# Second MoE of a three-stage kernel: one branch over two experts, the small second product ahead of it, row loads on another queue, small tiles at other addresses

## The chip, the cores and the metric

The kernel runs as one program on one core of one Trainium2 chip. The metric is device time in microseconds (us), from the first to the last instruction of one execution; lower is better. Of the core's engines five matter here: TensorE (PE, matrix products; PEld is its loading of weights), VectorE (DVE), ScalarE (ACT), GpSimd (POOL, which also issues the indirect DMAs) and SyncE (SP, which here issues the plain DMAs). Each engine runs its own list of instructions in order, branches included, and engines wait for each other through semaphores.

## The reference, cut to what matters

The program computes three things in a row: linear attention, a dense mixture of experts (every token through all eight experts), and a second mixture of experts with routing. Only the last is changed.

```
def _moe2_ref(x, w_gate, w1, w2, capacity):          # N 1152 tokens, D 512, E 8, F 1024, capacity 288
    logits = x @ w_gate
    expert_idx = np.argmax(logits, axis=1)
    ...                                              # gate_w: softmax probability of the expert taken
    for i in range(N):                               # the first `capacity` tokens of an expert get a slot
        e = expert_idx[i]
        if counts[e] < capacity:
            disp[e, counts[e]] = x[i]
            ...
    h = np.maximum(np.einsum('ecd,edf->ecf', disp, w1), 0.0)
    y = np.einsum('ecf,efd->ecd', h, w2)
    for i in range(N):
        if keep[i]:
            out[i] = gate_w[i] * y[expert_idx[i], pos[i]]
```

## The kernel before, in words

The first two stages keep TensorE busy and leave the tokens in the SBUF tile `acc` (128 x 9 x 520 values). Routing then writes each token's row, with its gate and its number behind it, to a DRAM buffer `disp` of 8 x 288 slots: nine indirect DMAs that POOL issues (L723), with the slot numbers in the small tile `slot_i`. They read `acc` and `slot_i` until they have landed. A bit mask `many` says which experts have more than 32 tokens.

The second MoE treats each expert in two parts. The small part takes the first 32 slots of an expert and always runs, in four steps for each expert. `first_small` (L1048, 32 matmuls) multiplies the 32 rows by w1; `relu_small` (L1056, ACT) applies the ReLU into a tile `g`; `turn_small` transposes (L1062, 2 matmuls) and copies (L1064, DVE) into `h`; `second_small` (L1072, 64 matmuls) multiplies by w2. Then `out_small` (L1079, ACT) scales by the gate, and `rows_out` (L1030, POOL) scatters the result to the output. The rows of four experts lie together in one tile: for experts 0 to 3 it is built before this stage, for experts 4 to 7 it is loaded by `slots_load` (L900) and transposed by `slots_trans` (L1020).

The large part, `large`, takes slots 32 to 287 of an expert and runs only under a branch on that expert's bit (`tc.If`, L1172). It loads 2 x 128 rows (`rows_load`, L1025), transposes them (L1100, 8 matmuls), and splits rows and weights into a high and a low part (ACT cast L80, then DVE subtract L81). The first product is 96 matmuls (L1113), the second 48 (L1130 to L1132), and ACT and DVE scale the two halves (L1138, L1136). Before the change the branch has two sides, and `second_small` is in both: inside `large`, behind the transposes of the rows, and alone in the other side. The loop over experts runs `turn_small(e)`, `out_small(e-1)`, `first_small(e+1)`, the branch of e, `relu_small(e+1)`. In the profiled data the experts 2 and 6 have more than 32 tokens; the other six skip the large part.

The weights come as 64 pieces of 512 KB (`load`, L535, on SP's queue), eight for each expert. There is room for 36 pieces; `done(e)` gives back the eight places of expert e, and the next `load(64)` fills all that are free.

The order is written out by hand: in this stage each engine runs its instructions as the code lists them. What sets the order is therefore the order of the lines, and a tile's address decides what its first writer waits for: a tile laid where an older tile lay waits for that tile's last readers.

Of the kernel before, what the change touches and what calls it, by code (L numbers as in the profile page):

```python
# [16 lines left out]
P = 128  # L17
# [3 lines left out]
def tile_linear_attention_two_moe(  # L21
# [507 lines left out]
    def load(n):  # L529

        while n and todo and free:
            e, i = todo.pop(0)
            src = piece(e, i)
            raws[e, i] = take((e, i), list(src.shape), F32, f"rw_{e}_{i}")
            nc.sync.dma_start(raws[e, i], wst[e, i].rearrange("p (c f) -> p c f", c=src.shape[1]))  # L535
            n -= 1

    def done(e):
        free.extend(at[e, i] for i in range(8))
# [455 lines left out]
    def bank2(k, name):  # L995
        return psum2[k].tile([P, 512], F32, tag="ps", name=name)
# [8 lines left out]
    NQD = P // C0  # L1005
    DQ = D // NQD
    tails0 = yp.tile([P, E, RW - D], F32, name="tails0")
    part = yp.tile([P, 1], F32, name="part")
    where = yp.tile([P, E], I32, name="where")
    out_q = out.rearrange("n (j d) -> (n j) d", j=NQD)  # L1010

    def slots_load(p):
        xs = yp.tile([P, D], F32, tag="xs", bufs=1, name=f"xs_{p}")
        rows_of_slots(p, xs)
        return xs
# [6 lines left out]

    def rows_load(e, c0, n):
        xs = yp.tile([P, RW], F32, tag="xt", bufs=2, name=f"xs2_{e}_{c0}")
        nc.scalar.dma_start(xs[:n, :], disp[e * cap + c0 : e * cap + c0 + n, :])  # L1025
        return xs

    def rows_out(o, at_, y, n):
# [12 lines left out]
    def first_small(e):  # L1041
        ps = bank2(0, f"q1_{e}")[:, :FP]
        x = xTs[e // EP]
        es = slice(e % EP * C0, (e % EP + 1) * C0)
        for c in range(DC):
            for j in range(NQD):
                js = slice(j * C0, (j + 1) * C0)
                nc.tensor.matmul(  # L1048
                    ps[js], x[:, c, es], raws[e, c][:, 0, j * FP : (j + 1) * FP], start=c == 0, stop=c == DC - 1,
                    tile_position=(0, j * C0),  # L1050
                )
        return ps

    def relu_small(e, ps):
        g = yp.tile([P, FP], F32, tag="g", bufs=2, name=f"g_{e}")
        nc.scalar.activation(g, ps, AF.Relu)  # L1056
        return g
# [9 lines left out]
    def second_small(e, ps, h):  # L1067
        for f in range(F // P):
            q, t = f // NH, f % NH
            for j in range(NQD):  # L1070
                js = slice(j * C0, (j + 1) * C0)
                nc.tensor.matmul(  # L1072
                    ps[js], h[:, t, q * C0 : (q + 1) * C0], raws[e, DC + f // 2][:, f % 2, j * DQ : (j + 1) * DQ],
                    start=f == 0, stop=f == F // P - 1, tile_position=(0, j * C0),
                )

    def out_small(e, ps):
        y = yp.tile([P, DQ], F32, tag="y", bufs=3, name=f"y_{e}")
        nc.scalar.mul(y, ps, tails0[:, e, 0:1])  # L1079
        rows_out(out_q, where[:, e : e + 1], y, P)  # L1080

    def large(e, chunks, rows, second):

        c0, w = chunks[0][0], sum(n for _, n in chunks)
        at_ = [c - c0 for c, _ in chunks]
# [10 lines left out]
        for c in range(0, DC, 2):  # L1096
# [4 lines left out]
                        ps[:, k, at_[i] : at_[i] + n], rows[i][:n, (c + k) * P : (c + k + 1) * P], ident[:n, :n]  # L1101
                    )
            split(xh[:, c : c + 2], xl[:, c : c + 2], ps)
        second()
        for i in range(1, DC):
            split_w(i)

# [34 lines left out]

    SETS = [REST[i : i + 2] for i in range(0, len(REST), 2)]
    assert len(SETS) <= 1
    xTs = {0: xT}
    xs = slots_load(1)
    for i in range(NQD):
        nc.sync.dma_start(
            tails0[i * C0 : (i + 1) * C0], disp[:, D:].rearrange("(e s) d -> s e d", e=E)[:C0]
        )  # L1150
    load(64)
    for j in range(NQD):
        nc.gpsimd.memset(part[j * C0 : (j + 1) * C0], float(j))
    g = relu_small(0, first_small(0))
    late = None
    for e in range(E):
        h = turn_small(e, g)
        if e == 0:
            wf = yp.tile([P, E], F32, name="wf")
            nc.vector.tensor_copy(wf, tails0[:, :, 1].bitcast(I32))  # L1160
            nc.vector.tensor_scalar(wf, wf, float(NQD), part[:, 0:1], ALU.mult, ALU.add)
            nc.vector.tensor_copy(where, wf)
        if e:
            out_small(e - 1, late)

        q = first_small(e + 1) if e + 1 < E else None
        late = bank2(0, f"q2_{e}")[:, :DQ]
        if REST:
            tc.no_sync_barrier()
            if e == 0:  # L1170
                mask = nc.values_load(many[0:1, 0:1], min_val=0, max_val=(1 << E) - 1)
            with tc.If(mask & (1 << e)) as more:  # L1172
                for chunks in SETS:
                    rows = [rows_load(e, c0, n) for c0, n in chunks]
                    large(e, chunks, rows, lambda: second_small(e, late, h))
            with more.Else():
                second_small(e, late, h)
        else:
            second_small(e, late, h)
        if q is not None:  # L1180
            g = relu_small(e + 1, q)
        if e % EP == 0 and e // EP + 1 < E // EP:
            xTs[e // EP + 1] = slots_copy(e // EP + 1, xqp, [slots_trans(e // EP + 1, xs)])
        if e:

            done(e - 1)
            load(64)
    out_small(E - 1, late)
    manual.close()


# [53 lines left out]
```

## Time and profile before

| | us |
|---|---|
| median of three runs (lowest, highest) | 1041.02 (1039.25, 1041.88) |
| the profiled execution, whole | 1043.93 |
| its span, first to last instruction | 1042.2 |
| PE busy in the span | 988.1 |
| DVE, ACT, POOL busy | 658.9, 342.7, 455.2 |

Busy time is summed over the whole span, most of which belongs to the first two stages, where PE is busy nine tenths of the time or more in nearly every slice. In the last slices, the second MoE, it is not. A row of the timeline below reads: start, duration, engine, line of the kernel, operation, output tile <- input tiles, shapes, and how many instructions the row merges; in brackets the time that the engine was idle just before, and what ended it. "issue" means that the profile shows nothing that the engine waited for.

### The profile page before, as it was taken

How to read it: one execution, taken by the hardware profiler on the slowest of the kernel's cores; microseconds unless marked ns; L12 is line 12 of the kernel's file. 1: busy time of each engine (PE TensorE's matmuls, PEld its weight loads, DVE VectorE, ACT ScalarE, POOL GpSimd, SP SyncE). 2: the span in 40 equal slices, each digit the busy share in tenths (PEclk: the TensorE clock that was granted, in tenths of full speed). 3: DMA queues.
4: the chain of work that ended last, by engine and by line, in shares of the span. 5: the costliest groups of instructions: out<-in, count | busy, mean ns of one | idle time of the engine just before them, and what ended most of it. 6: DMA issues, size and time to landing. Idle time of an engine off the chain costs nothing. (4 is left out here: it accounts for less than half of the span.)

```text
span 1042.2 us, 17368 instructions
## 1 busy us (share of the span) xinstructions
PE 988.1 (95%) x6686; PEld 889.5 (85%) x6686; DVE 658.9 (63%) x1288; ACT 342.7 (33%) x768; POOL 455.2 (44%) x480
## 2 busy tenths in 40 slices
PE   7999999999999999999999999999999999658586
PEld 7999989889998899988998889998999888537465
DVE  6766699997666666666666666666666665314041
ACT  5766553323222232332222223232223212113031
POOL 3656887646544445455544444445553300200101
PEclk9999999999999999999999999999999999868998
DMA  8888789841111111111111111111111164685500
GB/s 261 279 280 276 248 296 329 310 152 61 41 42 41 41 42 41 60 43 60 43 42 42 41 41 41 43 60 46 56 41 62 61 212 173 213 299 170 189 25 27
DMA packets 59873, 125.73 MB, mean 121 GB/s; under 512 B 6969, under 2 KB 25789, under 8 KB 59264
## 3 DMA queue, kind: packets, MB, share of 16 engines
q1 hardware_dynamic: 57904, 120.72, 34.2%
q0 software_dynamic: 1296, 2.63, 0.7%
q8 instruction: 64, 1.05, 0.4%
q10 hardware_dynamic: 576, 1.07, 0.3%
q14 instruction: 33, 0.27, 0.1%
HBM read 114.61 MB, written 44.68 MB: 153 GB/s over the span
## 5 line engine op out<-in xcount | busy, mean ns | idle before, releaser
L81 POOL TENSOR_TENSOR l<-r,h 128x256 fp32r<-128x256 f32 (+2 forms) x100 | 155.1, 1566 | 335.7 <-ACT h L80 335.7
L614 DVE SCALAR_TENSOR_TENSOR acc<-p,prob,acc 128x512 f32<-128x512 f32 x252 | 188.3, 749 | 103.0 <-PE p L605 102.9
L605 PE MATMUL p<-h,hl 128*128 128x512 f32 x576 | 226.6, 393 | 0.0
L603 PE MATMUL p<-h,hh 128*128 128x512 f32 x576 | 226.3, 393 | 0.0
L604 PE MATMUL p<-l,hh 128*128 128x512 f32 x576 | 225.1, 391 | 0.0
L569 DVE TENSOR_TENSOR ca<-ca,p 128x256 f32<-128x256 f32 (+1 forms) x256 | 113.0, 450 | 69.9 <-PE p L552 67.5
L80 ACT CAST h<-r 128x256 fp32r<-128x256 f32 (+2 forms) x108 | 70.8, 685 | 180.3 <-PE p L605 159.3
L558 ACT ACTIVATE hh<-ca 128x320 fp32r<-128x320 f32 (+1 forms) x128 | 56.3, 443 | 223.0 <-DVE ca L569 223.0
L605 PEld LDWEIGHTS p<-h,hl 128*128 128x128 f32 x576 | 108.2, 188 | 23.5 <-DVE hl L562 0.2
L604 PEld LDWEIGHTS p<-l,hh 128*128 128x128 f32 x576 | 108.2, 188 | 21.7
L603 PEld LDWEIGHTS p<-h,hh 128*128 128x128 f32 x576 | 108.3, 188 | 20.4
L81 POOL TENSOR_TENSOR lt<-t,ht 128x256 fp32r<-128x256 f32 x144 | 124.3, 891 | 1.3 <-PE pn L352 1.3
L550 PE MATMUL p<-xh,ht 128*128 128x320 f32 x256 | 79.2, 309 | 0.0
L552 PE MATMUL p<-xh,lt 128*128 128x320 f32 x256 | 79.1, 309 | 0.0
L551 PE MATMUL p<-xl,ht 128*128 128x320 f32 x256 | 79.1, 309 | 0.0
L550 PE MATMUL p<-xs,ht 128*128 128x256 f32 x256 | 72.8, 284 | 0.0
L552 PE MATMUL p<-xs,lt 128*128 128x256 f32 x256 | 72.4, 283 | 0.0
L551 PE MATMUL p<-xs,ht 128*128 128x256 f32 x256 | 72.4, 283 | 0.0
L569 DVE TENSOR_TENSOR cb<-cb,p 128x320 f32<-128x320 f32 (+1 forms) x128 | 58.1, 454 | 18.9 <-PE p L552 18.1
L562 DVE SCALAR_TENSOR_TENSOR hl<-ca,hh 128x320 fp32r<-128x320 f32 (+1 forms) x128 | 63.3, 496 | 2.3 <-ACT hh L558 1.5
L219 POOL TENSOR_TENSOR t<-r 128x256 f32<-128x256 f32 x72 | 54.8, 783 | 22.5 <-DMA r<-w1a 21.9
L562 DVE SCALAR_TENSOR_TENSOR hl<-cb,hh 128x512 fp32r<-128x512 f32 (+1 forms) x64 | 53.8, 841 | 11.0 <-ACT hh L558 11.0
(234 smaller groups left out, 2032.4 us busy)
## 6 DMA issues: line engine op xcount, KB each, us to landing
rw<-wst SPq DMA_DIRECT2D x64, 512.0 KB, 5.6
r<-w1a SPq DMA_DIRECT2D x36, 512.0 KB, 3.5
r<-w2a SPq DMA_DIRECT2D x36, 512.0 KB, 3.5
wst<-w1b SPq DMA_DIRECT2D x32, 512.0 KB, 7.1
wst<-w2b SPq DMA_DIRECT2D x32, 512.0 KB, 7.7
disp<-acc SPq DMA_DIRECT2D x18, 260.0 KB, 4.9
v<-va SPq DMA_DIRECT2D x8, 325.0 KB, 3.9
rawq<-qT SPq DMA_DIRECT2D x8, 320.0 KB, 5.6
```

The source lines that it names most:

```text
L80: nc.scalar.copy(hi, src)
L81: (eng or nc.vector).tensor_tensor(lo, src, hi, ALU.subtract)
L550: nc.tensor.matmul(ps, ws_[0], xs[0], start=i == 0, stop=False)
L551: nc.tensor.matmul(ps, ws_[0], xs[1], start=False, stop=False)
L552: nc.tensor.matmul(ps, ws_[1], xs[0], start=False, stop=i == DI - 1)
L558: nc.scalar.activation(hv[:, q0 : q0 + 2 * src.shape[1] - 1 : 2], src, AF.Relu)
L562: nc.vector.scalar_tensor_tensor(lv[:, qs], src, 0.0, hv[:, qs], ALU.max, ALU.subtract)
L569: nc.vector.tensor_tensor(o, x, ps, ALU.add)
L603: nc.tensor.matmul(ps, a, w.w2[0][:, f, :], start=f == 0, stop=False)
L604: nc.tensor.matmul(ps, a, w.w2[1][:, f, :], start=False, stop=False)
L605: nc.tensor.matmul(ps, b_, w.w2[0][:, f, :], start=False, stop=f == FT - 1)
L614: nc.vector.scalar_tensor_tensor(o, ps, prob[:, t, e : e + 1], o, ALU.mult, ALU.add)
```

## The change

Five edits, all in the second MoE. Five tiles `hi_0` to `hi_4`, used only by the large part, are now allocated before the small tiles, so that they take the addresses at which `acc` lay and the small tiles come behind. `rows_load` issues from SP instead of ACT. The loads of the first weights and the first product now stand ahead of the loads that read `disp`. `second_small` runs ahead of the branch, once. And the branch is now a tree: after every second expert one branch tests the bits of both, and inside it one branch for each runs its large part; places are given back, and weights loaded, once for a group of two.

```
+    for k in range(5):
+        yp.tile([P, 2 * D], R32, tag=f"hi{k}", bufs=1, name=f"hi_{k}")
 ...
-        nc.scalar.dma_start(xs[:n, :], disp[e * cap + c0 : e * cap + c0 + n, :])
+        nc.sync.dma_start(xs[:n, :], disp[e * cap + c0 : e * cap + c0 + n, :])
 ...
-    def large(e, chunks, rows, second):
+    def large(e, chunks, rows):
 ...
-        second()
         for i in range(1, DC):
             split_w(i)
 ...
+    GROUP = 2
     xTs = {0: xT}
+    load(64)
+    g = relu_small(0, first_small(0))
     xs = slots_load(1)
 ...
-    load(64)
 ...
-    g = relu_small(0, first_small(0))
-    late = None
+    late = {}
     for e in range(E):
         h = turn_small(e, g)
-        if e == 0:
+
+        q = first_small(e + 1) if e + 1 < E else None
+        late[e] = bank2(1, f"q2_{e}")[:, :DQ]
+        second_small(e, late[e], h)
+        if q is not None:
+            g = relu_small(e + 1, q)
+        if e == 1:
 ...
-        if e:
-            out_small(e - 1, late)
-
-        q = first_small(e + 1) if e + 1 < E else None
-        late = bank2(0, f"q2_{e}")[:, :DQ]
-        if REST:
-            tc.no_sync_barrier()
-            if e == 0:
-                mask = nc.values_load(many[0:1, 0:1], min_val=0, max_val=(1 << E) - 1)
-            with tc.If(mask & (1 << e)) as more:
-                for chunks in SETS:
-                    rows = [rows_load(e, c0, n) for c0, n in chunks]
-                    large(e, chunks, rows, lambda: second_small(e, late, h))
-            with more.Else():
-                second_small(e, late, h)
 ...
-        if e % EP == 0 and e // EP + 1 < E // EP:
+        if e % EP == 1 and e // EP + 1 < E // EP:
             xTs[e // EP + 1] = slots_copy(e // EP + 1, xqp, [slots_trans(e // EP + 1, xs)])
-        if e:
-
-            done(e - 1)
-            load(64)
-    out_small(E - 1, late)
+        if (e + 1) % GROUP == 0:
+            group = range(e + 1 - GROUP, e + 1)
+            for k in group:
+                out_small(k, late.pop(k))
+            if REST:
+                tc.no_sync_barrier()
+                if group[0] == 0:
+                    mask = nc.values_load(many[0:1, 0:1], min_val=0, max_val=(1 << E) - 1)
+                with tc.If(mask & sum(1 << k for k in group)):
+                    for k in group:
+                        tc.no_sync_barrier()
+                        with tc.If(mask & (1 << k)):
+                            for chunks in SETS:
+                                large(k, chunks, [rows_load(k, c0, n) for c0, n in chunks])
+
+            if group[0]:
+                for k in group:
+                    done(k - GROUP)
+                load(64)
```

The kernel after has five lines more; a line of the stage has grown by three (L1048 is L1051 now, L1072 is L1075), inside `large` by two or three (L1113 is L1115, L1100 is L1103).

The first place is PE at the start of the second MoE. In these rows `q_0`, `q_1` and `q_2` of L1048 are first products of experts 0, 1 and 2, `ht` a transpose, `q_0` of L1072 the second product of expert 0. Before, from the transpose of expert 0 to the one of expert 1 (the rows of `large` between the two branches left out):

```order
L1062 MATMUL ht_9853<-ident,g_9851 128x128 x2
L1048 MATMUL q_1_9862<-rw_0_9089,xT_9777 32x256 x4
...
L1171 TENSOR_LOAD many
L1172 REGISTER_ALU
L1172 COMPARE_AND_BRANCH
...
L1172 UNCONDITIONAL_BRANCH
L1072 MATMUL q_0_9879<-rw_4_9081,h_9856 32x128 x8
...
L1172 UNCONDITIONAL_BRANCH
L1020 MATMUL xst_10192<-ident,xs_9817 128x128 x4
L1062 MATMUL ht_10199<-ident,g_10190 128x128 x2
```

After, from the same transpose to the first branch:

```order
L1065 MATMUL ht_9858<-ident,g_9843 128x128 x2
L1051 MATMUL q_1_9863<-rw_0_9089,xT_9777 32x256 x4
...
L1075 MATMUL q_0_9880<-rw_4_9081,h_9861 32x128 x8
...
L1065 MATMUL ht_9915<-ident,g_9913 128x128 x2
L1051 MATMUL q_2_9920<-rw_0_9271,xT_9777 32x256 x4
...
L1075 MATMUL q_1_9937<-rw_4_9097,h_9918 32x128 x8
...
L1023 MATMUL xst_9976<-ident,xs_9845 128x128 x4
L1182 TENSOR_LOAD many
L1183 REGISTER_ALU
L1183 COMPARE_AND_BRANCH
```

The small work of two experts, and the first product of a third, now stands in one piece ahead of the first branch.

The second place is ACT at the same point, with the semaphores that each row waits for. `g` is the result of the ReLU; the semaphores DMASW0 to DMASW7 are counted up by POOL's indirect DMAs, here the scatters into `disp`. Before, the first three rows of the small part:

```order
L1056 ACTIVATE g_9851<-q_0_9834 128x256 [waits DMASW3_49,DMASW4_49,DMASW2_49,DMASW5_49,DMASW1_49,DMASW6_49,DMASW0_49,DMASW7_49,DVE_49,PE_49]
L1171 TENSOR_LOAD many [waits DVE_49]
...
L1056 ACTIVATE g_10190<-q_1_9862 128x256 [waits PE_49]
```

After:

```order
L1059 ACTIVATE g_9843<-q_0_9826 128x256 [waits DVE_49,PE_49]
L1059 ACTIVATE g_9913<-q_1_9863 128x256 [waits DMASW3_49,DMASW4_49,DMASW2_49,DMASW5_49,DMASW1_49,DMASW6_49,DMASW0_49,DMASW7_49,DVE_49,PE_49]
L1059 ACTIVATE g_9970<-q_2_9920 128x256 [waits PE_49,Activation_49]
```

The wait for all scatters has moved from the first `g` to the second, whose tile lies over `slot_i`.

The third place is SP's queue around the first loads of the stage. `rw` is a piece of the weights, `xs` (L900) and `tails` the rows and the gates read from `disp`, `xs` (L1025, L1028) the rows of a large part. Before, up to the first loads behind a branch:

```order
L535 DMA rw_1_9602<-wst 128x1024
L900 DMA xs_9817<-disp 32x512 x4
L1148 DMA tails_9814<-disp 32x8x8 x4
L535 DMA rw_2_9826<-wst 128x1024
L535 DMA rw_3_9828<-wst 128x1024
...
L1172 UNCONDITIONAL_BRANCH x2
L535 DMA rw_4_10525<-wst 128x1024
```

After (the rows of the first group left out):

```order
L535 DMA rw_1_9602<-wst 128x1024
L535 DMA rw_2_9822<-wst 128x1024
L535 DMA rw_3_9824<-wst 128x1024
L900 DMA xs_9845<-disp 32x512 x4
L1154 DMA tails_9814<-disp 32x8x8 x4
...
L1028 DMA xs_2_32_10631<-disp 128x520
L1028 DMA xs_2_160_10633<-disp 128x520
...
L535 DMA rw_4_11083<-wst 128x1024
L535 DMA rw_5_11085<-wst 128x1024
```

The two pieces that fill the room now go ahead of the reads of `disp`, and the rows of expert 2 ahead of the sixteen pieces that replace experts 0 and 1.

## Rows read from the trace of the kernel before

**Rows 1.** Groups by line from 925 us on: busy, mean ns, idle before.

```profile
L1072 PE MATMUL q<-rw,h 128*32 128x128 f32 x448 | 22.3, 369 | 21.3 <-issue 20.7 <-DVEq L1172 0.6
```

**Rows 2.** Timeline of PE, start of the second MoE: start, duration, idle before.

```profile
898.10 1.93 PE L1048 MATMUL q<-rw,xT 128*32 128x256 f32 x32
906.70 0.69 PE L1062 MATMUL ht<-ident,g 128*128 128x128 f32 x2 [6.67 <-ACT g L1056]
907.32 3.16 PE L1048 MATMUL q<-rw,xT 128*32 128x256 f32 x32
912.88 2.01 PE L1072 MATMUL q<-rw,h 128*32 128x128 f32 x36 [2.40 <-DVE wf L1160]
917.98 1.92 PE L1072 MATMUL q<-rw,h 128*32 128x128 f32 x28 [3.08 <-issue]
919.83 1.12 PE L1020 MATMUL xst<-ident,xs 128*128 128x128 f32 x4
928.86 3.64 PE L1072 MATMUL q<-rw,h 128*32 128x128 f32 x64 [4.55 <-issue]
```

**Rows 3.** Timeline of PE, from expert 2 to the large part of 6.

```profile
940.64 0.66 PE L1100 MATMUL xst<-ident,xs 128*128 128x128 f32 x2 [5.34 <-DMA xs<-disp]
...
970.52 0.44 PE L1062 MATMUL ht<-ident,g 128*128 128x128 f32 x2 [0.35 <-ACT g L1056]
...
978.39 3.46 PE L1072 MATMUL q<-rw,h 128*32 128x128 f32 x64 [5.57 <-issue]
...
998.03 3.15 PE L1072 MATMUL q<-rw,h 128*32 128x128 f32 x64 [2.96 <-issue]
...
1006.09 1.96 PE L1072 MATMUL q<-rw,h 128*32 128x128 f32 x64
1007.97 0.39 PE L1113 MATMUL q<-xh,hi 128*128 128x256 f32 x1
```

**Rows 4.** Timeline of ACT: the first ReLU, and the large part of 6.

```profile
906.26 0.38 ACT L1056 ACTIVATE g<-q 128x256 f32<-128x256 f32 x1 [8.22 <-DMA disp<-acc,slot_i]
...
1001.22 0.37 ACT L1079 ACTIVATE y<-q,tails 128x128 f32<-128x128 f32 x1 [5.64 <-PE q L1072]
1001.73 0.98 ACTq L1025 DMA_DIRECT2D xs<-disp  x2
1002.75 1.04 ACT L80 CAST hi<-rw 128x1024 fp32r<-128x1024 f32 x1 [1.17 <-DVE h L1064]
...
1030.03 0.69 ACT L1138 ACTIVATE y<-q,xs 128x512 f32<-128x512 f32 x1 [9.86 <-PE q L1132]
```

**Rows 5.** Timeline of DVE: expert 0's gates, and the large part of 6.

```profile
912.71 0.17 DVE L1160 CAST wf<-tails 128x8 f32<-128x8 int32 x1 [4.86 <-DMA tails<-disp]
...
1003.83 1.23 DVE L81 TENSOR_TENSOR rw<-rw,hi 128x1024 fp32r<-128x1024 f32 x1 [1.57 <-ACT hi L80]
1006.38 1.29 DVE L81 TENSOR_TENSOR xl<-xst,xh 128x512 fp32r<-128x512 f32 x2 [1.32 <-ACT xh L80]
...
1031.52 0.42 DVE L1064 COPY h<-ht 128x256 f32<-128x256 f32 x1
```

**Rows 6.** Timeline of POOL, the end.

```profile
1032.28 0.98 POOL L1030 DMA_INDIRECT out<-y,xs  x1 [0.30 <-DVEq L1172]
...
1038.18 0.97 POOL L1030 DMA_INDIRECT out<-y,where  x1 [3.65 <-ACT y L1079]
```

**Rows 7.** Windows: us, busy (instructions) of five engines, PEclk, DMA share, GB/s.

```profile
928.86:932.50 3.64, 3.64 (x65) 3.26 (x66) 0.00 (x0) 0.00 (x0) 0.00 (x0) 0.50 0.57 171
1006.09:1008.05 1.96, 1.96 (x66) 1.76 (x65) 1.53 (x3) 1.96 (x4) 0.00 (x0) 1.00 0.04 8
936.00:940.00 4.00, 0.00 (x0) 0.00 (x0) 0.51 (x1) 0.00 (x0) 0.00 (x0) 1.00 1.00 385
956.00:960.00 4.00, 4.00 (x31) 3.79 (x30) 2.40 (x4) 2.40 (x4) 0.00 (x0) 1.00 0.43 134
```

**Rows 8.** Waits of SP's queue from 880 us on: total, times, longest.

```profile
SPq L535 <- PE q L1113: 14.6, 4, 7.3
```

More of the change, by code (lines that the diff above doesn't have):

```diff
@@ L1162, in tile_linear_attention_two_moe @@
             nc.vector.tensor_copy(where, wf)
-        if e:
-            out_small(e - 1, late)
-        q = first_small(e + 1) if e + 1 < E else None
-        late = bank2(0, f"q2_{e}")[:, :DQ]
-        if REST:
-            tc.no_sync_barrier()
-            if e == 0:
-                mask = nc.values_load(many[0:1, 0:1], min_val=0, max_val=(1 << E) - 1)
-            with tc.If(mask & (1 << e)) as more:
-                for chunks in SETS:
-                    rows = [rows_load(e, c0, n) for c0, n in chunks]
-                    large(e, chunks, rows, lambda: second_small(e, late, h))
-            with more.Else():
-                second_small(e, late, h)
[L1178 to L1181, printed above, removed]
-        if e % EP == 0 and e // EP + 1 < E // EP:
-            xTs[e // EP + 1] = slots_copy(e // EP + 1, xqp, [slots_trans(e // EP + 1, xs)])
-        if e:
-            done(e - 1)
-            load(64)
-    out_small(E - 1, late)
+        if e % EP == 1 and e // EP + 1 < E // EP:
+            xTs[e // EP + 1] = slots_copy(e // EP + 1, xqp, [slots_trans(e // EP + 1, xs)])
+        if (e + 1) % GROUP == 0:
[16 more added lines that the diff above has]
+                load(64)
     manual.close()
```

## Prediction

> **What bounds the kernel now.** I read the slices of the page first: PE is full until the last seventh of the span, so the change can only be worth something there. Next the timeline of PE in that stretch, for its idle times, and the timelines of ACT, DVE and POOL for who ends them.
>
> The stage starts when PE has finished the first product of expert 0, at 898.10 + 1.93 = 900.03 us, and ends with the span at 1042.2: 142 us. In it two large parts of some 22 us each keep PE full (from 1007.97 to ACT's first scaling at 1030.03 is 22.06) [rows 3, 4]; most of the rest is small work with PE waiting. The waits are of four kinds.
>
> - The scatters. PE sits idle 6.67 us before the first transpose [rows 2], because ACT's ReLU waits until 906.26 for the DMAs that read `acc` and `slot_i` [rows 4].
> - The skipped branches. Each time an expert's large part is skipped PE finds its next matmul late: 2.40 + 3.08 for expert 0 and 4.55 for expert 1 [rows 2], 5.57 for expert 3, 2.96 for expert 5 [rows 3]. From 925 us on such waits sum to 20.7 us [rows 1]; 20.7 - 4.55 - 5.57 - 2.96 = 7.6 is left for experts 4 and 7. No other engine ends them. Where the branch is taken there is none: in expert 6 the second product runs unbroken into the first row of the large one, 1006.09 + 1.96 to 1007.97 [rows 3].
> - The rows of a large part: 5.34 us for expert 2 [rows 3].
> - The end: the large part of 6 is over at 1030, and expert 7, with one more skip, lies behind it until POOL's last DMA at 1038.18 [rows 6].
>
> PE's clock adds to this. [...]
>
> **The change part by part.** I follow PE through the new order. One small expert is a transpose, a first product and a second: 0.44 + 1.93 + 1.96 = 4.33 us at full clock [rows 2, 3], 0.69 + 3.16 + 3.64 = 7.49 at half [rows 2].
>
> *Small tiles at other addresses.* The order of ACT shows that only the first `g` is freed of the scatters; the second now waits for all of them. So from 900.03 the work of expert 0 runs (0.6 for the ReLU and its handoffs, then 4.33) to 905.0, and the transpose of expert 1 stands where that of expert 0 stood, at 906.70. The two weight pieces that now go ahead of the reads of `disp` share the DMA engines with the scatters: 2 x 0.524 MB at 385 GB/s [rows 7] is at most 2.7 us, at least 0; I take 1.0, since most of the scatters are issued before. That gives 907.7. Then transpose, first and second product, and the transposes of the other rows (1.12 [rows 2], 0.65 by the clock): 5.0 at full, 8.6 at half clock; 6.8 between them: 914.5. The gates and rows from `disp`, there at 912.7 before [rows 5], come at 913.7 and are not later than PE.
>
> *The first branch*, skipped for both experts: 2.96 to 5.48 by the skips above; near expert 0's, which also loads the mask, but with fewer weights under way: 4.5. To 919.0. Here two skips and their cold restarts have become one.
>
> *Experts 2 and 3, small.* Two experts at 4.33, with the first piece behind the gap at half clock as after 928.86 (+1.7, and 0.25 for the transpose): 10.6. To 929.6. The rows of expert 2 cost nothing: SP issues them when PE, ACT, DVE and POOL are past the first branch, about 920, and no weights are ahead of them; if that cover went, the 5.34 would come back.
>
> *Start of the large part.* `second_small` used to fill PE while ACT and DVE split rows and weights; now it is done before, and the splits are bare. From PE's last matmul: 0.1 to ACT's scaling, 1002.75 - 1001.22 - 0.98 (the two DMA issues that leave ACT) = 0.55 to the first cast, 1.04 for it, 1.23 for DVE's subtract, 0.65 for half of the rows' [rows 4, 5], three handoffs of 0.1: 3.8 us, of which PE works 1. At half clock the first products add 0 to 1.7; I take 0.8. So this edit costs, 4.6 against 1.96 for each large part. To 934.2, and with 22.06 + 0.7 for the second half to 956.9.
>
> *The skip of expert 3*, now inside the taken branch. Nearest is the same expert's 5.57; against it stands the jump at the end of a taken branch, over the other side, after which PE was idle only 0.35, for ACT [rows 3]. Bounds 0 and 5.6; taken 4.3: 961.2.
>
> *Experts 4 and 5, small*, 10.6: 971.8. *Their branch*, skipped, 2.96 to 5.6, taken 4.0: 975.8. *Experts 6 and 7, small*: 4.33, then 0.44 + 1.96 as no first product is left, 0.6 for the copy into `h` that nothing covers now (0.42 [rows 5] and handoffs), 1.9 for the clock: 9.2, to 985.0. The large part of 6: 4.6 + 22.06, so ACT scales at 1011.7.
>
> *The end.* Before, 2.25 us from that scaling to POOL's second DMA of the large part, and 4.0 from POOL's last DMA to the end of the span [rows 4, 6]: 6.3, to 1018.0. Expert 7's skip, 3 to 6 us on each engine, lies beside the landing.
>
> *Weights.* They are given back by twos. Sixteen pieces (8.4 MB) go out at about 920; at 385 GB/s they are in after 22 us, 942, and are first needed at 961. The other twelve follow as the large part of 2 frees their places, the last after 956.9, and are needed from 976. Nothing, then; the price if not is a rival below.
>
> The sum is 1018.0 - 1042.2 = -24.2 us within the profiled execution, whose whole time, 1043.93, is 2.9 above the median of the runs. On the median: 1041.0 - 24.2 = 1016.8, say 1017. Most of it: fewer skips (5.48 + 21.3 = 26.8 us of waits [rows 1, 2] to three of 12.8 in sum), small work at full clock, and the tail.
>
> [...] In the rows each skip of one large part cost 2.96 us or more, and the taken branch of expert 6 nothing [rows 2, 3]. [...]
>
> **The rivals.**
>
> *Each skip pays twice.* Expert 0's did, 2.40 and again 3.08 in the middle of its matmuls [rows 2], and a skip inside a taken branch ends in a second jump, over the outer branch's other side. Three times 2.5 to 3.1: 1017 + 8 = 1025. Against: experts 1, 3 and 5 show one wait only.
>
> *The skips are cheap and the clock stays up*: waits of 2.96, 0 and 2.96 (-6.9), and half of the clock's terms gone (1.8 + 3 x 1.9 + 2 x 0.8 = 9.1, half 4.5): 1006. For it: the shortest wait stands where no weights move; against: most others were longer.
>
> *The waits are not the branch's* but the second product's, where all of them show: then they stay, 26.8 instead of 12.8: 1031. Against: the second products of experts 2 and 6, inside taken branches, have none.
>
> *The weights come late*: slower. SP's queue holds the rows of expert 2 until four engines have passed the first branch, and sixteen pieces behind them. At the 134 GB/s of 956 to 960 [rows 7] these last 63 us, to 982, and the other twelve 47 more, to 1029; expert 7 needs the last, and then the large part of 6 follows: 1029 + 2 + 26.7 + 6.3 = 1064, a span 22 us longer than before. It decides from the rate at which the last piece lands about 1005, 28 x 0.524 MB in 85 us: below 170 GB/s the change loses. Against: in that slow stretch SP was waiting for places, 14.6 us for PE's first product alone [rows 8]; with places free it ran at 385.
>
> *The change doesn't do what it says*: the second `g` waits in the sum already. If the first did too, the work of expert 0 would start at 906.70: +4.3, 1021, within the range.
>
> **How the numbers follow.** Forecast 0.51; twice-paying skips 0.20; cheap skips 0.17; waits not the branch's 0.06; weights late 0.04; no gain for a reason I don't see 0.02. The forecast's own range is 1008 to 1027 (skips -4 and +4, clock -5 and +6). With the two next cases the range is 1003 to 1030, which leaves out some 2 in 10. A difference below 0.3%, about 3 us, is what a measurement of this kernel can't tell from none. Faster: all but the last two cases, 0.93; within 0.3%: 0.03; slower 0.04.
>
> **What would show it.** Three waits of PE of 3 to 5.5 us without a releaser between 905 and the last large part, none in the small work of a group; ACT's second ReLU, not the first, ending a wait for the scatters, near 907; the rows of a large part landed before PE asks; some 3 us of idle PE before each first product of a large part, ended by ACT and DVE; the last DMA of POOL being that of the large part of 6. The forecast is wrong if a DMA of weights ends a wait of PE, if small work waits within a group, or if the skip inside the taken branch costs over 6 us.

## The result, and the profile after

The changed kernel takes 1012.51 us (median of four runs, 1008.50 to 1013.36) against 1040.13 (1038.32 to 1041.88) for the kernel before, run beside it: a ratio of 0.9727, 95% interval 0.9694 to 0.9760, so 28 us less. The forecast was 1017, with 1003 to 1030 as its range. In the profiled execution (1013.31 us whole) the span went from 1042.2 to 1011.5; the work ahead of the second MoE takes the same time in both, and lines in this part of the code have moved down by three.

First the groups by line from 895 us on (busy, mean ns of one, idle before and what ended it), which answer to [rows 1]:

```profile
L1115 PE MATMUL q<-xl,hi 128*128 128x256 f32 x64 | 18.9, 296 | 2.0 <-DVE xl L81 2.0
L1115 PE MATMUL q<-xh,hi 128*128 128x256 f32 x64 | 18.9, 295 | 2.8 <-ACT xh L80 2.8
L1075 PE MATMUL q<-rw,h 128*32 128x128 f32 x512 | 16.8, 281 | 0.8 <-DVE h L1067 0.5 <-issue 0.3
L1065 PE MATMUL ht<-ident,g 128*128 128x128 f32 x16 | 3.9, 334 | 12.8 <-PEq L1183 8.6 <-ACT g L1059 3.7 <-PEq L1186 0.4
```

The waits without a releaser (20.7 us from 925 us on) are gone from the second product: 0.3 us is left, beside 0.5 for DVE. What is left of the skips stands before the transposes behind a branch, and now has a name, PE's own sequencer (PEq) at the lines of the branch: 8.6 + 0.4 us. New are 2.8 + 2.0 us ahead of the large part's first product.

The same along time, PE's timeline, for [rows 2, 3]:

```profile
897.86 1.93 PE L1051 MATMUL q<-rw,xT 128*32 128x256 f32 x32
903.53 0.69 PE L1065 MATMUL ht<-ident,g 128*128 128x128 f32 x2 [3.74 <-ACT g L1059]
...
913.26 0.63 PE L1023 MATMUL xst<-ident,xs 128*128 128x128 f32 x4 [0.38 <-DMA xs<-disp]
918.11 0.66 PE L1065 MATMUL ht<-ident,g 128*128 128x128 f32 x2 [4.22 <-PEq L1183]
...
926.79 1.93 PE L1075 MATMUL q<-rw,h 128*32 128x128 f32 x64
928.65 1.09 PE L1103 MATMUL xst<-ident,xs 128*128 128x128 f32 x8
931.52 0.38 PE L1115 MATMUL q<-xh,hi 128*128 128x256 f32 x1 [1.78 <-ACT xh L80]
932.89 0.38 PE L1115 MATMUL q<-xl,hi 128*128 128x256 f32 x1 [0.99 <-DVE xl L81]
...
957.51 0.44 PE L1065 MATMUL ht<-ident,g 128*128 128x128 f32 x2 [0.43 <-PEq L1186]
...
970.80 0.41 PE L1065 MATMUL ht<-ident,g 128*128 128x128 f32 x2 [4.41 <-PEq L1183]
...
981.41 0.38 PE L1115 MATMUL q<-xh,hi 128*128 128x256 f32 x1 [1.04 <-ACT xh L80]
```

ACT's timeline, for [rows 4]:

```profile
903.10 0.38 ACT L1059 ACTIVATE g<-q 128x256 f32<-128x256 f32 x1 [5.29 <-remote]
907.95 0.38 ACT L1059 ACTIVATE g<-q 128x256 f32<-128x256 f32 x1 [4.47 <-DMA disp<-acc,slot_i]
...
929.58 0.37 ACT L1082 ACTIVATE y<-q,tails 128x128 f32<-128x128 f32 x1 [1.83 <-issue]
929.93 1.04 ACT L80 CAST hi<-rw 128x1024 fp32r<-128x1024 f32 x1
...
1004.80 0.69 ACT L1140 ACTIVATE y<-q,xs 128x512 f32<-128x512 f32 x1 [9.87 <-PE q L1134]
```

The second ReLU, not the first, waits for the scatters. The first is late all the same: PE's product ends at 899.79 by its row, the ReLU starts 3.3 us later, and "remote" says that the trace can't name what released it. The cast of the first weight, which opens the large part, stands behind the scaling of expert 3's rows. The end, POOL's timeline, for [rows 6]: the large part of 6 is now last.

```profile
1007.05 0.97 POOL L1033 DMA_INDIRECT out<-y,xs  x1 [0.30 <-issue]
```

Windows (us, busy of PE, PEld, DVE, ACT, POOL, granted clock, DMA share, GB/s), from the first small product to the span's end; of before, and then of after with two slices in which the weights move, for [rows 7]:

```profile
898.10:1042.20 144.10, 97.66 (x1092) 75.76 (x1092) 33.17 (x46) 29.84 (x47) 15.21 (x20) 0.84 0.43 147
```

```profile
897.86:1011.50 113.64, 88.83 (x1092) 70.34 (x1092) 32.67 (x46) 29.74 (x47) 15.15 (x20) 0.91 0.54 192
...
930.00:940.00 10.00, 7.49 (x48) 7.29 (x49) 8.99 (x9) 8.58 (x10) 0.97 (x1) 0.83 1.02 410
940.00:950.00 10.00, 10.00 (x70) 9.19 (x69) 4.15 (x6) 2.40 (x4) 0.00 (x0) 1.00 1.01 402
```

The stretch is 30.5 us shorter. The same 1092 matmuls took 8.8 us less, since the granted clock was 0.91 in place of 0.84; the other 21.6 us are PE's idle time (46.4 before, 24.8 after). No DMA of weights ends a wait of PE.

### The profile page after: what moved, and what is told of

It is laid out like the page before. It is cut to its first block, busy times and chain, and to the rows that moved or that the text cites. A ratio compares the mean times of both kernels' runs of the same rounds, so it can differ in the third digit from the quotient of the medians.

```text
span 1011.5 us, 17383 instructions
## 1 busy us (share of the span) xinstructions
PE 979.7 (97%) x6686; PEld 884.4 (87%) x6686; DVE 658.4 (65%) x1288; ACT 342.7 (34%) x768; POOL 456.0 (45%) x480
## 5 line engine op out<-in xcount | busy, mean ns | idle before, releaser
L605 PEld LDWEIGHTS p<-h,hl 128*128 128x128 f32 x576 | 108.2, 188 | 23.5 <-DVE hl L562 0.2
L604 PEld LDWEIGHTS p<-l,hh 128*128 128x128 f32 x576 | 108.2, 188 | 21.7
L603 PEld LDWEIGHTS p<-h,hh 128*128 128x128 f32 x576 | 108.3, 188 | 20.4
```

The costliest lines, as they stand in the source:

```text
L603: nc.tensor.matmul(ps, a, w.w2[0][:, f, :], start=f == 0, stop=False)
L604: nc.tensor.matmul(ps, a, w.w2[1][:, f, :], start=False, stop=False)
L605: nc.tensor.matmul(ps, b_, w.w2[0][:, f, :], start=False, stop=f == FT - 1)
```

## The experiments

All are edits of the changed kernel. Times are medians; the ratio, with its 95% interval, is to the kernel before run beside it, and the changed kernel's is 0.9727. "Idle" and "busy" are PE's, in the window from the first small product to the span's end of one profiled execution. The kernel before was run anew with each group (its medians lie between 1038.3 and 1040.1), so a difference of two medians here is good to some 2 us; the ratios are the measure.

| | us | ratio | window | busy | idle | clock |
|---|---|---|---|---|---|---|
| changed kernel | 1012.51 | 0.9727 (0.9694, 0.9760) | 113.6 | 88.8 | 24.8 | 0.91 |
| e1 branch for each expert | 1022.87 | 0.9851 (0.9825, 0.9877) | 124.5 | 94.6 | 29.9 | 0.88 |
| e11 and product inside | 1027.41 | 0.9897 (0.9879, 0.9914) | 125.8 | 90.4 | 35.5 | 0.90 |
| e3 dead code | 1011.00 | 0.9734 (0.9707, 0.9761) | 111.3 | 88.0 | 23.4 | 0.92 |
| e4 ballast | 1013.30 | 0.9755 (0.9729, 0.9781) | 113.6 | 93.3 | 20.4 | 0.93 |
| e2 no reserve | 1012.40 | 0.9754 (0.9724, 0.9783) | 112.2 | 87.2 | 25.0 | 0.92 |
| e6 rows on ACT | 1018.69 | 0.9798 (0.9770, 0.9825) | 118.8 | 91.8 | 27.1 | 0.89 |
| e5 ACT shift | 1019.76 | 0.9796 (0.9769, 0.9824) | 115.7 | 90.9 | 24.8 | 0.90 |
| e10 three scatters | 1005.5 (one run) | - | 106.4 | 84.2 | 22.2 | 0.96 |
| e7 front | 1014.85 | 0.9766 (0.9738, 0.9794) | 111.4 | 85.3 | 26.0 | 0.93 |
| e8 front, ACT shift | 1021.16 | 0.9814 (0.9787, 0.9841) | 115.4 | 88.3 | 27.1 | 0.91 |
| e9 front, six tiles | 1002.85 | 0.9644 (0.9615, 0.9673) | 101.2 | 83.7 | 17.5 | 0.96 |
| e12 front, singles | 1009.27 | 0.9718 (0.9700, 0.9735) | 108.2 | 85.9 | 22.2 | 0.94 |

### What a skip costs: e1, e11, e3, e4

**e1**, the tree undone:

```
-    GROUP = 2
+    GROUP = 1
-        if e == 1:
+        if e == GROUP - 1:
             wf = yp.tile([P, E], F32, name="wf")
```

> The changed kernel with a branch for each expert again (a group of one), its second product of small chunks still outside the branch. Theory (each branch that TensorE skips costs a refill of its instruction stream): TensorE meets skips at experts 0, 1, 3, 4, 5 and 7 in place of the first pair, 3, the third pair and 7, so two refills more of 2.96 to 4.4 us each: 6 to 9 us above the changed kernel, 1018.5 to 1021.5 us, and four waits of 2.9 to 4.5 us at the branch's line on TensorE ahead of the products of experts 1, 2, 5 and 6. Rival (the second product outside the branch did it all, the pair's tree nothing: a skip of one large part, half as long, is free as that of expert 3 was): 1010.5 to 1014.5 us and waits under 1 us at the branches.

The time came out 1.4 us above the theory's range, but not by the waits it named. PE's timeline at the branches:

```profile
908.68 0.41 PE L1065 MATMUL ht<-ident,g 128*128 128x128 f32 x2 [0.49 <-PEq L1183]
...
914.88 0.44 PE L1075 MATMUL q<-rw,h 128*32 128x128 f32 x4 [3.92 <-DVEq L1183]
...
962.51 0.41 PE L1065 MATMUL ht<-ident,g 128*128 128x128 f32 x2 [0.93 <-PEq L1183]
...
972.34 0.66 PE L1065 MATMUL ht<-ident,g 128*128 128x128 f32 x2 [4.43 <-PEq L1183]
...
979.46 0.41 PE L1065 MATMUL ht<-ident,g 128*128 128x128 f32 x2 [0.19 <-PEq L1183]
```

Of four expected waits of 2.9 to 4.5 us one is there (expert 4, 4.43); experts 0, 3 and 5 cost 0.49, 0.93 and 0.19. At expert 1 PE waits 3.92 us for DVE, which had to wait for the gates ahead of expert 0's branch and was then held 0.90 us at that branch itself. Both readings fell: skips of one part are neither all dear nor all free. The trace also has a row for each branch on PE's own sequencer. There the branches of experts 0, 3, 4 and 5 take 0.36, 1.64, 5.00 and 0.44 us, so the difference lies in the branch. The 10 us come from elsewhere too: 5.1 us are idle (expert 2's rows 3.6, DVE 3.9, less from skips), 5.7 us are busy time at a clock of 0.88.

**e11**, e1 with the product back in both arms:

```
-        late[e] = bank2(1, f"q2_{e}")[:, :DQ]
-        second_small(e, late[e], h)
+        late[e] = bank2(0, f"q2_{e}")[:, :DQ]
+        with tc.If(mask & (1 << e)) as more:
+            ...  large(e, chunks, [...], lambda: second_small(e, late[e], h))
+        with more.Else():
+            second_small(e, late[e], h)
```

> The first experiment's version (a branch for each expert) with the second product of the small chunk back inside both arms of the branch, behind the first splits of the large part in the one; the rows still on SP's queue, the first product still ahead of the slots' load, the small tiles still off acc's place. Theory (a product behind the branch starts only when TensorE has its stream again, and the arm that it stands in makes every skip longer by its own 128 instructions): each of the skips at experts 0, 1, 3, 4 and 5 costs TensorE 2.4 to 5.6 us, as in the kernel before, in place of the 0.2 to 4.4 us of the version with the product outside, 6 to 12 us in all: 1029 to 1035 us. Rival (the place of the product doesn't matter, the refill is the same): 1021 to 1025 us.

```profile
906.26 2.35 PE L1075 MATMUL q<-rw,h 128*32 128x128 f32 x36 [5.13 <-issue]
...
915.65 1.95 PE L1075 MATMUL q<-rw,h 128*32 128x128 f32 x64 [2.19 <-issue]
...
962.15 3.10 PE L1075 MATMUL q<-rw,h 128*32 128x128 f32 x64 [3.90 <-issue]
...
972.95 2.69 PE L1075 MATMUL q<-rw,h 128*32 128x128 f32 x43 [5.06 <-issue]
981.43 0.82 PE L1075 MATMUL q<-rw,h 128*32 128x128 f32 x21 [2.22 <-issue]
```

Between the two expectations: 1027.41, 0.5% above e1. The waits do come back in the size of the kernel before, 18.5 us in these five rows against 6.0 at PEq in e1, so the product's place matters, by 4.5 us in the medians. The window shows less of it: PE was busy 4.2 us less than in e1, the first ReLU was not late in this trace (below), and the profiled execution was the fastest of its six.

**e3**, the part of expert 3, which never runs, made longer, so that its skip is as long as that of a pair:

```
-        for c in range(DC):
+        for c in [*range(DC)] * (3 if e == 3 else 1):
```

> The changed kernel with 192 more matmuls in the large part of expert 3, which is skipped: they never run. The skip of expert 3 was nearly free (0.43 us at the branch). Theory A (TensorE's sequencer runs ahead of its queue of long matmuls, so that the refill falls under the end of expert 2's large part): still under 1 us at that branch, 1012 to 1014 us. Theory B (the target of that skip lay in what was fetched already, since the skip is short): the skip is now some 700 instructions long like that of a pair, and the wait becomes 2.9 to 4.5 us: 1015.5 to 1017.5 us.

```profile
956.07 0.44 PE L1065 MATMUL ht<-ident,g 128*128 128x128 f32 x2 [0.44 <-PEq L1186]
```

Theory A for PE's wait: 0.44 us, as before. But the branch itself did get longer. On PE's sequencer the test of expert 3 takes 0.34 us in the changed kernel (953.18 to 953.52), and 3.52 here (951.68 to 955.20), with one packet of the DMA queue that the profile calls instruction in that time. PE's matmuls, queued ahead, ran until 955.63 and hid all of it. So in the changed kernel this skip was free twice over: the branch over one part didn't wait, and if it had, the large part of expert 2 would have hidden it.

**e4**, long matmuls ahead of a dear skip:

```
+                if group[0] == 4:
+                    bal = bank2(1, "ballast")
+                    for _ in range(6):
+                        nc.tensor.matmul(bal, ident, raws[5, 0][:, 0, :512], start=True, stop=True)
                 tc.no_sync_barrier()
```

> The changed kernel with six matmuls of 128x128 by 128x512 in fp32, whose result is not used, on TensorE just ahead of the third pair's branch (experts 4 and 5, 4.41 us of wait at the skip). [...] Theory A (the sequencer runs ahead of long matmuls and the refill falls under them): the wait at the branch's line falls from 4.4 to under 1.5 us and the kernel is 1 to 2.5 us slower than the changed kernel. Theory B (the refill starts only when the work ahead has ended, or depends on the distance alone): the wait stays at 4 to 4.5 us and the kernel is 5 us slower, 1017.5 us.

```profile
963.30 5.42 PE L1183 MATMUL ballast<-rw,ident 128*128 128x512 f32 x12
968.87 0.41 PE L1065 MATMUL ht<-ident,g 128*128 128x128 f32 x2
```

Theory A again: the ballast took 5.42 us, the wait of 4.41 behind the branch is gone, and the kernel is 0.8 us above the changed one by the medians (3 by the ratios, whose intervals overlap), not 5. The ballast did not shorten the branch: here it occupies PE's sequencer from 963.36 to 968.55, with two packets of the instruction queue in that time, and the ballast runs from 963.30 to 968.72. In the changed kernel the same branch takes from 965.67 to 970.63, with nothing queued after 966.39. So in e4 the whole branch runs while PE still works on what was queued, and the skip costs PE only what its queue doesn't cover. Small matmuls at the full clock (64 in 1.93 us) covered 0.7 us of that branch in the changed kernel and nothing of the first pair's; the ballast covered all 5.19 us. Both theories' times rest on a length for the ballast that no run had shown before this one. The branches here of 3.5 us and more (e3's, e4's, expert 4's in e1, both pairs' in the changed kernel) each have an instruction packet moving in their time, and those of 0.34 to 0.44 us have none. That a long branch waits for such a packet, a refill, is my reading; the traces name neither what the branch waits for nor the engine that a packet is for. What they do show is that the wait is paid only where PE runs dry: 4.41 us in the changed kernel, none here.

### The other edits: e2, e6

**e2**: the two lines with `hi_0` to `hi_4` taken out.

> The changed kernel without the two lines that reserve the place of acc for the large part's weights, so that the small tiles lie there again. Theory: the first ReLU stays free of the scatters, but expert 0's turned tile then waits for all five (some 908 us in place of 904.3), its second product starts at about 908.5, and since the transposes of the slots' rows wait for their load until 913.3 anyhow, 1 to 1.5 us of it are left at the first branch: 1013.5 to 1014 us. Rival (nothing waits in between, each wait adds up): 4 us, 1016.5 us. Second rival (what the first ReLU waits for in the changed kernel, 3.2 us after its product's end, is something else than data; if it stays late here too, it isn't the place).

```profile
908.02 1.95 PE L1072 MATMUL q<-rw,h 128*32 128x128 f32 x64 [1.15 <-DVE h L1064]
```

The mechanism is the theory's (DVE's copy into `h` waits for the scatters until 907.54), the size smaller: 1.15 us, after which the wait for the slots' rows is gone. The time doesn't differ: the reservation is worth nothing that these runs can tell. The first ReLU is late by the same 3.3 us.

**e6**: `nc.sync.dma_start` in `rows_load` back to `nc.scalar.dma_start`.

> The changed kernel with the large part's two row loads back on ScalarE's queue. Theory (their issue stands ahead of the weight casts in ScalarE's stream, some 1 us by the prediction's working, and the loads start only when ScalarE has skipped the first pair and made the row results): TensorE's transposes of expert 2's large part wait for the rows, which come 4 us after an issue at about 929.6, so 5 to 6 us at expert 2 and 4 to 5 us at expert 6, and the kernel is 8 to 11 us slower than the changed one: 1020.5 to 1023.5 us. Rival (SP's queue gives nothing, since the loads are short): 1 us per large part, 1014.5 us.

```profile
928.49 0.52 PE L1103 MATMUL xst<-ident,xs 128*128 128x128 f32 x2 [3.93 <-DMA xs<-disp]
...
983.96 1.35 PE L1103 MATMUL xst<-ident,xs 128*128 128x128 f32 x4 [3.41 <-DMA xs<-disp]
```

The waits are the theory's, a little short (4.2 and 3.4 us in place of 5 to 6 and 4 to 5). While PE waits for rows the first weight is cast, so the bare splits of the changed kernel (2.8 and 2.0 us) vanish under them, and the time is 6 us above it, not 8 to 11. Of the 5.2 us by which the window grew, 2.2 are idle and 2.9 are busy time at a lower clock (0.89). Rows on SP's queue are worth these 6 us.

### The late first ReLU: e5, e10

**e5**:

```
+    for k in range(3):
+        nc.scalar.copy(const.tile([P, 1], F32, name=f"pad_{k}"), ones[:, 0:1])
```

> The changed kernel with three copies of one column on ScalarE at the kernel's start, whose results nothing reads; they move all later ScalarE instructions two places on in its program (one semaphore instruction falls away). In the changed kernel the first ReLU begins 3.3 us after its product's end, in every trace of it and of its variants so far. Theory (ScalarE's instruction stream has the edge of a fetched block just before this ReLU): the edge now falls two instructions earlier, into ScalarE's idle stretch ahead of the copy of the slots' rows, the copy is at most 0.5 us later and the ReLU begins within 0.3 us of its product's end. Rival (it waits for something of its data or its engine): it stays 3.3 us late. The time hardly gains by it in either case, 1009.5 to 1012.5 us, since the second ReLU still waits for the scatters (908), the second half of the slots' rows for its load (913.3) and the first pair's rows for the tails (914.7).

ACT's timeline, and a row of the page's groups of this kernel and of the changed one:

```profile
908.42 0.38 ACT L1061 ACTIVATE g<-q 128x256 f32<-128x256 f32 x1 [5.23 <-remote]
```

```profile
L603 PE MATMUL p<-h,hh 128*128 128x512 f32 x576 | 228.9, 397 | 0.0
```

```profile
L603 PE MATMUL p<-h,hh 128*128 128x512 f32 x576 | 226.3, 393 | 0.0
```

The theory fell: the ReLU is as late as ever. That instructions come in packets is in the page of the changed kernel (59 on queue q8, 0.97 MB); that the edge of one lay just before this ReLU no trace shows, it was my estimate. And the kernel lost 7 us, far ahead of the changed code: in the first MoE 1728 matmuls (this row and two like it) take 684.1 us in place of 678.0. What the edit changes ahead of that stage are three short ScalarE instructions and the three tiles they write, which may move the tiles allocated behind them. Which of these is the cause was not shown.

**e10**: `for t in self.ts[: 3 if self.n == 5 else None]` in the scatter.

> The changed kernel, with the last two of the five scatters of the second half of the tokens left out (their rows stay empty; all later work is the same). In nine traces the end of TensorE's first small product, as the ReLU that waits for it shows it, stood 1.1 to 1.2 us behind the end of GpSimd's last scatter issue, whatever the product's own start was. Theory (the product is held until GpSimd has issued its scatters): GpSimd is done 2.55 us earlier, and the ReLU starts 2.5 us earlier, 2.7 us after the product's start in place of 5.24. Rival (it is tied to something ahead of the scatters, the route or the weights' transfers): 5.2 us after the product's start as before.

```profile
899.41 0.38 ACT L1059 ACTIVATE g<-q 128x256 f32<-128x256 f32 x1 [2.05 <-PE q L1051]
```

The ReLU came 2.0 us after the product's start, earlier than the theory's 2.7, with no delay left. But e9, e11 and e12, with all five scatters, have none either (2.0 to 2.1 us), while the changed kernel, e1 to e5 and e8 have 5.2 to 5.3 and e6 and e7 3.9 to 4.0. In the nine late traces it starts 1.1 to 1.2 us behind the end of POOL's last scatter issue, in e11 and e12 2.0 us ahead of that end. e1 and e11 are alike up to there. So neither a place in ACT's program nor the scatters alone explain it. There is one trace of each kernel, and the nine late ones were all taken before the other four, so it isn't known whether the kernel or the execution decides; the cause stays open.

### A better version: e7, e8, e9, e12

**e7** moves what stood ahead of the large parts. Its core:

```
+        if e % GROUP == 0:
+            q2 = bank2(1, f"q2_{e}").rearrange("p (k d) -> p k d", d=DQ)
+        late[e] = q2[:, e % GROUP]          # a bank of their own, for two experts
...
+        if e == 2:                          # gates and the slots' second half, used only now
+            wf = ...
+            xTs[1] = slots_copy(1, xqp, [slots_trans(1, xs)])
...                                          # behind the branch of experts 2 and 3, and of 4 and 5:
+            elif group[0]:
+                outs()                      # out_small for all that wait
```

> A version meant to be better, on the changed kernel: the results of the second small products lie in banks of their own (two experts in one), so that their scaling and their writes go behind the branch of the second pair (in the last pair behind the first casts of the large part, or in the other arm); the register with the mask is loaded behind the first product; the slots' second load and its transposes are used at expert 2, and the tile lies where expert 1's ReLU doesn't collide with the scatters. Theory (what held the start of expert 2's large part was the chain scatters, slots' load, tails, and each large part then waited 2 to 2.8 us for its first casts behind the row results): the first ReLU still starts 3.3 us late, the first dense product of expert 2 begins at 925 to 927.5 in place of 932.9, the gap of TensorE ahead of it is under 1.2 us in both large parts, and the time is 1003 to 1006 us. Rival (the rows of expert 2 reach TensorE no earlier, since SP skips the first pair in 3.5 us and their load takes 4 us, landing at 922): the gain is at most 4 us, 1008.5 us.

ACT's timeline behind expert 2's large part, and PE's at its start and behind it:

```profile
951.44 0.88 ACT L1077 ACTIVATE y<-q,tails 128x128 f32<-128x128 f32 x3 [0.42 <-DMA rw<-wst]
963.00 0.37 ACT L1077 ACTIVATE y<-q,tails 128x128 f32<-128x128 f32 x1 [10.67 <-DMA out<-y,where]
963.26 0.37 ACT L1054 ACTIVATE g<-q 128x256 f32<-128x256 f32 x1
```

```profile
928.60 0.39 PE L1111 MATMUL q<-xl,hi 128*128 128x256 f32 x1 [0.34 <-DVE xl L81]
...
963.69 0.69 PE L1060 MATMUL ht<-ident,g 128*128 128x128 f32 x2 [7.88 <-ACT g L1054]
```

The front came out nearly as the theory had it: the dense product that stood at 932.89 starts at 928.60 (the theory said 925 to 927.5), with gaps of 0.3 + 0.3 us before both large parts. The time, 1014.85, missed theory and rival alike, since the gain was given back at once: four scalings in a row found three tiles `y`, the fourth waited 10.67 us for the first one's rows to be written out, and the next ReLU, and PE, stood behind it.

**e8** is e7 with the three copies of e5:

> The version before with the three copies at ScalarE's start as well. Theory (the first ReLU's block edge is gone and nothing else holds TensorE before the first pair's branch): 3 us below the version without them, 1000 to 1003 us. Rival (the rows of expert 2 land no earlier than 922, so the start of its large part stays): within 1 us of the version without them.

It was 6 us slower, by the same longer matmuls of the first MoE (684.1 us); it tells nothing new on the ReLU, which is late in it.

**e9** is e7 with `tag="y", bufs=6`:

> The version with the second products' results in banks of their own, with six small result tiles in place of three. In the version with three, ScalarE's fourth row result behind expert 2's large part waited 10.7 us until the first one's rows had been written out (962.9), and TensorE stood 7.9 us for the ReLU behind it. Theory: that wait goes, TensorE's gap after expert 4's product is under 1 us, the skip of the third pair stays at 3 to 4.5 us, and the time is 7 to 8 us under the version with three, 1006.5 to 1008.5 us, 4 to 6 us under the changed kernel. Rival (the rows out and the weights share the DMA queues, and something else on that path waits as long): over 1011 us.

```profile
915.08 0.66 PE L1060 MATMUL ht<-ident,g 128*128 128x128 f32 x2 [3.73 <-PEq L1193]
...
927.69 0.39 PE L1111 MATMUL q<-xl,hi 128*128 128x256 f32 x1 [0.34 <-DVE xl L81]
...
950.50 0.44 PE L1060 MATMUL ht<-ident,g 128*128 128x128 f32 x2 [0.43 <-PEq L1214]
...
963.29 0.66 PE L1060 MATMUL ht<-ident,g 128*128 128x128 f32 x2 [4.46 <-PEq L1193]
...
973.59 0.39 PE L1111 MATMUL q<-xl,hi 128*128 128x256 f32 x1 [0.34 <-DVE xl L81]
```

12 us under e7, more than the 7 to 8 expected, and 9.7 us under the changed kernel (8.6 by the ratios): the best version here. The wait of 7.88 is gone, the three skips cost as much as in the changed kernel (3.73, 0.43 and 4.46; 3.39, 0.50 and 2.92 in e7), and with fewer stops the clock is 0.96. Some 2 us between e7 and e9 are the ReLU's, late in the one trace and not in the other.

**e12** asks whether e9 does better with single branches for experts 0 to 5:

> The best version so far (results in banks of their own, six result tiles, 1002.85 us) with a branch for each of experts 0 to 5 and the pair only for 6 and 7; the weights' loads stay where they were. Theory (a skip of one large part is cheap when it comes alone, under 1 us, and dear when a second one follows it within one small expert's work, 4.4 us, as at experts 0, 3, 5 and at 4 in the first experiment): TensorE waits under 1 us at experts 0, 3 and 5 and 3.5 to 4.5 us at 1 and 4, the sum is that of the pairs, 1001 to 1005 us. Rival A (every short skip is cheap once nothing else waits): 995 to 998 us. Rival B (every skip costs a refill): 1008 to 1012 us.

PE's timeline at its five skips (experts 0, 1, 3, 4, 5):

```profile
906.06 0.41 PE L1060 MATMUL ht<-ident,g 128*128 128x128 f32 x2 [2.37 <-PEq L1193]
913.02 0.41 PE L1060 MATMUL ht<-ident,g 128*128 128x128 f32 x2 [1.29 <-PEq L1193]
...
951.01 0.66 PE L1060 MATMUL ht<-ident,g 128*128 128x128 f32 x2 [2.83 <-PEq L1193]
960.58 0.41 PE L1060 MATMUL ht<-ident,g 128*128 128x128 f32 x2 [4.06 <-PEq L1193]
967.46 0.41 PE L1060 MATMUL ht<-ident,g 128*128 128x128 f32 x2 [1.17 <-PEq L1193]
```

6.4 us slower than e9, at 1009.27 between the theory's range and rival B's: 11.7 us of skips in place of 8.6, and again no two alike. Expert 3's costs 2.83 here, with the rest of its small work between the large part and its branch, and 0.43 in e9, where it stands right behind the large part. On PE's sequencer the five branches take 2.91, 1.83, 3.38, 4.60 and 1.72 us, where e1's took 0.36 to 5.00 over jumps of one part as well: why one such jump is short and another long remains open. What is shown is that the pairs are faster than single branches, here and in e1; the waits at the skips make 3.1 of the 6.4 us here and none of the 10 in e1.

## Why the prediction was right, step by step, and where it was off

The forecast stood 6.5 us above the profiled span (1018.0 against 1011.5). Its steps:

- *To the first branch*: 914.5, measured 913.89, partly by luck. The second ReLU waits for the scatters as said (907.95), and the transpose behind it starts at 908.84, 1.1 us later than the forecast's 907.7. The stretch from there went by the full clock (1.00 granted) and took 5.1 us in place of 6.8, so the two errors cancel. That the first ReLU comes at once was wrong, by some 3 us; it cost nothing, since PE had to wait 0.38 us for the rows of the slots until 913.26, which the forecast held to be earlier than PE.
- *The first branch*: 4.5, measured 4.22. *Experts 2 and 3*: 10.6, measured 10.6 (918.11 to 928.72). *Rows and weights cost nothing*: so it is; e6 shows what the rows' cover is worth, 6 us.
- *Start and body of the large part*: 27.3 and 26.7 us to ACT's scaling, measured 27.7 and 25.5. The bare splits cost what was said (2.8 and 2.0 us idle); e9 shows that they needn't be bare (0.28 and 0.34 us there).
- *The skip of expert 3*: taken at 4.3, with 0 as its lower bound; PE waited 0.43. This is the term that was most mis-sized: counted from ACT's scaling it is 3.2 us of the 6.5. That a skip holds PE up was right for the pairs, whose branches take 3.97 and 4.96 us on PE's sequencer, each with an instruction packet moving in its time; the branch of expert 3 takes 0.34 us, with none. The sum also priced every skip by the jump and not by what PE had queued: e3 shows that a jump of twice the length, which does wait (3.52 us), is as free there, and e4 that another dear one becomes free behind long matmuls.
- *The waits before*: that no other engine ends them was read too broadly, since [rows 1, 2] name DVE for 2.40 and 0.6 us. For the 2.40 the reading holds even so: PE's branch of expert 0 takes from 908.89 to 912.72 in that trace, and the product starts at 912.88.
- *Experts 4 and 5*: 10.6, measured 8.9 (957.51 to 966.39): without the stop at expert 3 no half clock followed (1.00 granted, against 0.75 for experts 2 and 3). *Experts 6 and 7*: 9.2, measured 8.55. These, with the second large part, are the other 3.6 us.
- *The third branch*: 4.0, measured 4.41. *The end*: 6.3, measured 6.7, with the large part of 6 last.

The rivals: no skip pays twice in the changed kernel; the waits were the branch's, since they moved with it from the second product to the transposes; weights ran at 402 to 410 GB/s and were not late; "skips cheap and the clock up" (1006) was half right, for one skip of three.

Where the 28 us came from, by undoing parts, in ratios to the kernel before: with rows on SP, the first product ahead of the loads, the reservation and the new order of the small steps it is 0.9897 (e11); the product outside the branch makes it 0.9851 (e1); the tree over two makes it 0.9727. The tree is the largest step by the ratios (0.0124, against 0.0103 for e11's part, which the intervals don't separate), and not by the count of skips, as I had it: in e1 the waits at PEq were 6.0 us, less than the changed kernel's 9.0. It also takes a wait for the gates (3.9 us in e1) and one for expert 2's rows (3.6) off PE, keeps the clock up (0.91, against 0.88 in e1), and leaves no small work behind the last large part.

## What to carry to other kernels

A skipped branch took 3.5 us and more on PE's sequencer in the dear cases here and 0.3 to 0.4 in the cheap ones, and PE paid only where its queue ran dry (4.41 us in the changed kernel, nothing behind e4's 5.42 us of matmuls). Put the branch right behind long work, and try fewer branches over more code: that was faster in both comparisons here. When work is taken out of a gap that hid a transfer or a cast, look at once at what is now bare, and at the depth of each ring of tiles that the new order fills in one go. A small edit far ahead (e5) took back 7 of the 28 us; compare the untouched stages too.

## What the hardware showed that was not expected

- Six matmuls (12 records, 5.42 us) hid a whole skip: the branch behind them took 5.19 us on PE's sequencer, and PE's wait of 4.41 us was gone.
- Jumps over one large part took from 0.34 us (expert 3, changed kernel) to 5.00 (expert 4, e1) on PE's sequencer; what decides was not taken apart.
- Three one-column copies more, with their tiles, made 1728 matmuls of an untouched stage 0.9% longer (684.1 us against 678.0), in two kernels alike; the cause was not taken apart.
- The first small product, or what reports it to ACT, took 5.2 us in some traces and 2.0 in others of like programs; open.
